# A fused retention and feed-forward kernel: the order of its late tasks, with the transpose of tile 14's x ahead of that of q and k of tile 20

## The chip, the cores and the metric

The kernel runs on one core of one Trainium2 chip. A core has five engines that run side by side: TensorE (PE in the profile; its weight loads are PEld), VectorE (DVE), ScalarE (ACT), GpSimd (POOL) and SyncE (SP). Each takes its instructions in the order in which the program gives them, and an instruction that waits holds all that stand behind it on the same engine. SyncE, ScalarE and GpSimd also issue transfers, which the core's 16 DMA engines carry out. Matrix products land in PSUM, which has eight banks here, and everything else lives in SBUF. The metric is the time of one execution on the device in microseconds, the median of several runs.

## What is computed

The reference has two parts: a recurrence over 768 positions for each of 4 sequences and 8 heads, and a feed-forward network with a layer norm over the joined heads.

```
gamma = 1.0 - 2.0 ** (-5.0 - np.arange(H))          # one decay per head
for t in range(S):
    state = gamma * state + einsum('bhd,bhe->bhde', k[:, :, t], v[:, :, t])
    y[:, :, t] = scale * einsum('bhd,bhde->bhe', q[:, :, t], state)
x = y.transpose(0, 2, 1, 3).reshape(B, S, H * D)    # 4 x 768 x 512
xn = (x - mean(x)) / sqrt(var(x) + 1e-06) * g_ln
out = x + maximum(xn @ w_ch1, 0.0) @ w_ch2          # 512 -> 2048 -> 512
```

## The kernel before

The 4 x 768 positions are cut into 24 tiles of 128 positions. Tiles 0 to 3 are the first chunks of the four sequences; tiles 4 to 8, 9 to 13, 14 to 18 and 19 to 23 are the five further chunks of each sequence in turn. Within a tile the recurrence is a masked product: scores of q and k, times a mask of decays, times v. Across tiles a state is carried, which the chunks of k and v build up in bank PD.

The whole program is a list of some thousand tokens, the string `ORDER`. A token names one task, and the tasks are emitted in the order of the list. So the list fixes the order of work on each engine and, with it, the order of each engine's queue of transfers; all waits between engines follow from what the tasks read and write. The part of a token behind `/` names the engine where there is a choice (A ScalarE, D or nothing VectorE, S SyncE), the part behind `//` the banks. The tokens that matter here, with the line by which the profile names their instructions:

- `k`, `q`, `v` (L362): GpSimd issues the load of a tile's k, q or v, and the type changes from fp32 to bf16 on the way. q and k of tiles from 7 on have 8 slots, v has 9. `gk`, `gq`, `gv` (L391) are gates: GpSimd copies one element of the loaded tile, so that its queue goes on only when the load has landed. `vg` (L482): GpSimd multiplies v by decays.
- `tr` (L405): SyncE issues a transpose by DMA of q and k of a tile together; `ex` (L525): the same for the normalized x of a tile, half as large, from `xn` into `xnt`. Both stand in one queue. `eq` (L411): VectorE scales the transposed q.
- `vis` (L420 and L426): for two tiles at once TensorE computes the scores into the banks X0 to X3 and the share of the carried state into Y0 and Y1. `am` (L433): VectorE applies the mask, one bank each, which frees the bank. `py` (L448): TensorE multiplies the masked scores by v, into Y0 and Y1. `pd` (L490): TensorE adds k and vg into PD. `pb` (L501 on ScalarE, L505 on VectorE) reads the state off PD.
- `bn` (L456, L457), `sr` (L587), `rt` (L596), `nb` (L591), `xg` (L600), `xc` (L472): mean and variance, the root and its reciprocal, the shift, the normalized x, and a copy of x.
- `m` (L550): four blocks of x times w1 into a bank; `r` (L561 or L563): the relu that empties it. `wg` (L608 on ScalarE, L610 on VectorE): w1 times g_ln. For the groups of tiles 16 to 19 and 20 to 23 (numbers 12 and 13) the first product of the network is done with seven products in place of eight, in the manner of Strassen and Winograd: `wm` (L631) and `xt` (L653) make the sums of w1 and x, `f` (L671) the products, `fs` (L685) and `fo` (L698) their sums, and `fq` (L703) and `fr` (L712 on ScalarE, L710 on VectorE) the relu.
- `z` (L568): the second product of tiles 0 to 7, `ad` (L576) the sum with x. Tiles 8 to 23 do the second product two by two with seven products as well: `tm` (L620) are the four sums of blocks of w2, done once on VectorE in bf16 over 128 x 2048 elements, `sa` (L726) the sums of the hidden values, `s` (L737) the products and `o` (L751) their sums with x. `st` (L583): ScalarE issues the store of a tile.

Products are grouped by tiles: group 8 is tiles 8 and 9, group 9 tiles 10 and 11, group 10 tiles 12 and 13, group 11 tiles 14 and 15. `m11_8`, the first product of group 11, needs the transposes `ex14` and `ex15`. The queue of SyncE around it, as far as it is given by the list, is

```
ex15/S tr18 tr19 tr20 ex14/S ex16/S tr21 ex17/S ex19/S ex18/S tr22 tr23
```

and the queue of GpSimd from the last loads of tile 21 on is

```
q21 v22 vg21 vg20 gk21 q22 q23 gv20 gq21 vg22 k22 k23 v23
```

Of the kernel before, what the change touches and what calls it, by code (L numbers as in the profile page):

```python
# [47 lines left out]
z2_3 ad0 tr10 gq10 z3_0//M v12 gk11 st0/A ad2 z3_1 tr11 eq8 q13 vis8//X2,X1,X3,X0 tm1 z3_2 am8b am9a
pd9 z3_3 vg11/ pb10/A am8a m7_12//X1 am9b vg10/ ad3 py9 r7_12/A py8 q12 z4_0//M bn8 xc9a gv11 z4_1
xc8b bn9 k13 z4_2 xc9b sr8 sr9 z4_3 rt8 rt9 nb8 nb9 eq10 xg8a m7_8//X0 xg8b ad4 xc8a ex8/S xg9b pd10  # L50
gv12 z5_0//M gv10 xg9a pb11 gk12 q14 r7_8/A z5_1 ex9/S eq11 gq11 k15 wg2/D pd11 vis10//X0,X1,X2,X3
tr12 pb12/A k14 z5_2 am11a sq6 v14 tr13 wg3/A am11b z5_3 rs6 vg12/ am10a py11 m7_4//X2 am10b gq13
vg2/ ad5 py10 m6_4//X0 xc11b bn11 gq14 z6_0//M r6_4/A bn10 pd12 gk15 gk13 z6_1 gq12 v13 pb13 sr10
sr11 st1/A z6_2 q15 rt10 r7_4/A rt11 nb10 nb11 wg1/D xg11a z6_3 v15 xg11b xg10a m8_14//X0 ex11/S ad6
gk14 gv14 xc10b vg14/ xc10a m8_8//X1 xc11a xg10b tr14 v16 r8_14/A eq12 pd2 z7_0//M eq13 r8_8/A tm2
ex10/S pb14/A vis12//X0,X1,X2,X3 gv13 z7_1 wg0/A am12a am12b pd14 m8_4//X0 gq15 tr15 k16 am13a py12
am13b m8_6//X1 k17 sq7 bn12 r8_4/A m8_12//X2 q16 tm4 sr12 r8_6/A py13 m8_2//X0 q17 xc12a r8_12/A
rt12 bn13 m8_0//X1 vg15/ xc13a xc13b nb12 m8_10//X2 r8_2/A gv15 gv16 eq14 xc12b k18 sr13 z7_2 xg12a
rt13 rs7 nb13 pb15 r8_10/A v17 z7_3 xg13a vg16/ r8_0/A m9_8//X0 ad7 xg13b xg12b pd15 eq15 ex13/S
s8_1//M sa8_1 r9_8/A pb16/A vis14//X0,X1,X2,X3 ex12/S st2/A s8_5 am14b tr16 gk18 am15a pd16 q20  # L60
m9_0//X1 am14a gk17 m9_12//X2 gq17 am15b tr17 gv17 gk16 k20 tm3 py14 py15 m9_10//X0 q18 st3/A r9_0/A
sa8_3 m9_6//X3 q19 r9_12/A bn15 st6/A m9_2//X1 k19 r9_6/A sa8_2 s8_2//X2 bn14 vg3/ r9_2/A xc15a
m10_2//X3 r9_10/A sa8_4 vg17/ xc14a sr14 m9_14//X0 o8_1 sr15 xc14b gq20 r10_2/A rt14 nb14 s8_6 pb17
xc15b r9_14/A rt15 s8_3 o8_2 gq18 nb15 eq16 xg15a m10_14//X0 xg15b o8_3 eq17 xg14b ex15/S m9_4//X1
v19 o8_4 r10_14/A wm3 xg14a s8_7 gq16 tr18 r9_4/A st4/A v18 pd17 vis16//X0,X1,X2,X3 o8_5 pb18/A
sa10_1 tr19 gk19 v20 s8_4 am16b am16a pd3 m10_12//X1 am17a py16 st5/A am17b m10_4//X0 xc16b o8_6
# [2 lines left out]
r10_10/A m10_8//X0 nb16 gk20 eq18 xg16a rt17 s10_2//X1 o10_1 xg16b q21 xc16a nb17 sa10_4 ex16/S
xc17b s10_6 r10_8/A o10_2 v22 xg17b eq19 s10_3 xg17a sa12_1 vis18//X0,X1,X2,X3 o10_3 vg21/ o10_4  # L70
pd19 am19b s10_7 pb20/A vg20/ am18b m11_8//X3 am18a gk21 q22 o10_5 m11_6//X1 r11_8/A am19a q23
sa12_3 py18 py19 pd20 m11_14//X0 bn19 tr21 gv20 pb21/A gq21 vg22/ s10_4 bn18 sr19 ex17/S k22 pd21
m11_4//X2 rt19 o10_6 sr18 r11_6/A rt18 nb19 sa12_2 xc18b s12_1//M r11_4/A nb18 k23 wm2 xg19a s12_5
xg19b v23 xg18a eq20 m11_0//X1 ex19/S xg18b o12_1 xc19b s12_2//X2 sa12_4 xc19a ex18/S xc18a r11_0/A
wm4 s12_6 pb22/A s12_3 eq21 r11_14/A o12_2 pd22 o12_3 vis20//X0,X1,X2,X3 o12_4 tr22 s12_7 am20b
pb23/A am20a f12_1_1//X1 am21a m11_2//PD fs12_1_1 xt12_1 f12_0_1//X0 am21b f12_1_5//X2 xt12_2
fs12_0_1 py20 o12_5 py21 fs12_1_5 m11_12//X3 xt12_3 tr23 r11_2/A bn21 f12_1_6 r11_12/A f12_0_2//PD
bn20 fs12_1_2 f12_0_6 m11_10//X3 xc20b fo12_0_1 sr20 fs12_0_2 rt20 f12_1_7 xt12_4 sr21 xc20a nb20
f12_0_5//PD eq22 xg20a f12_0_7 fo12_1_3 fs12_0_5 s12_4 rt21 xc21a eq23 r11_10/A nb21 fo12_0_3
f12_1_4 xg21a f12_1_2//X3 o12_6 xg21b f12_1_3 sa14_1 xg20b f12_0_4 xc21b fo12_1_1 ex20/S f12_0_3  # L80
fq12_1 fo12_1_2 s14_1//M fq12_0 sa14_2 st13/A ex21/S vis22//X0,X1,X2,X3 st12/A fo12_0_2 s14_5 am22b
am23b f12_3_5//PD f12_3_1//X1 am23a f12_2_1//X3 am22a f12_2_5//X2 st9/A fs12_3_5 py23 sa14_4 py22
fs12_2_1 s14_2//X0 bn22 fs12_2_5 f12_2_6 fs12_3_1 bn23 f12_3_3 fs12_2_2 f12_2_3 sr22 f12_3_6 o14_1
sr23 fr12_1_2/A f12_2_7 rt22 rt23 fs12_3_2 s14_6 nb22 fo12_2_2 xg22b fo12_2_3 f12_3_7 xc22a xc22b
f13_1_1//X2 fo12_3_2 xc23a xg22a s14_3 o14_2 nb23 ex22/S fo12_3_3 xg23a f12_2_4 xg23b o14_3
f13_0_2//X0 sa14_3 xc23b f13_0_1//PD ex23/S fr12_0_1/A f12_2_2//Y0 o14_4 f12_3_4 fo12_2_1 st11/A
s14_7 fq12_3 fr12_0_2/D fs13_0_1 f12_3_2//Y0 o14_5 fr12_1_1/A f13_2_1//X1 fo12_3_1 f13_1_2//Y1
xt13_1 s14_4 fs13_1_1 xt13_2 st14/A xt13_3 f13_0_5//Y0 fq12_2 o14_6 f13_0_6 st10/A fo13_1_1
f13_2_2//X3 fs13_0_5 fr12_3_1/D f13_1_5//M fs13_0_2 fo13_0_1 f13_0_3 fs13_1_5 f13_1_6 fo13_0_2
fr12_2_1/A f13_0_7 f13_3_1//X0 fo13_0_3 fs13_2_1 f13_3_2//Y0 sa16_1 fr12_3_2/A f13_1_3 f13_3_5//Y1  # L90
fs13_1_2 xt13_4 f13_2_6 fo13_2_1 fs13_3_1 f13_1_7 fo13_3_1 f13_2_5//X3 f13_3_6 fo13_1_3 s16_1//Y0
fo13_1_2 fs13_3_5 sa16_3 fs13_2_5 s16_5 fr13_0_1/A sa16_2 f13_3_3 o16_1 f13_2_3 fs13_2_2 f13_1_4
fs13_3_2 fo13_2_2 f13_2_7 fr12_2_2/A f13_3_7 fr13_1_1/A s16_6 fo13_3_3 fq13_1 fr13_2_1/D s18_1//M
fo13_2_3 fr13_1_2/A f13_3_4 sa16_4 s16_2//X2 fq13_3 sa18_1 fr13_3_2/A s16_3 sa18_3 fr13_2_2/A sa18_2
f13_0_4 f13_2_4 fo13_3_2 fq13_0 s18_5 o16_3 fr13_3_1/A sa18_4 s18_2//X0 o16_4 fq13_2 o18_1 s16_7
st15/A o16_2 s18_6 st16/A o16_5 fr13_0_2/D o18_2 s20_1//Y1 sa20_1 s16_4 sa20_2 s20_5 s22_1//PD
sa22_1 o20_1 s18_3 o16_6 s20_6 st17/A o18_3 sa20_4 s22_5 sa22_2 s20_3 s20_2//X0 sa22_4 o18_4
s22_2//X1 o20_3 o22_1 s18_7 o22_2 s22_6 o18_5 sa20_3 s22_3 o20_4 sa22_3 s18_4 o22_3 o20_2 s20_7
# [753 lines left out]
```

## Time and profile before

| | us |
|---|---|
| median of 3 runs | 207.11 |
| the three runs | 206.81, 207.11, 210.05 |
| the profiled execution | 204.79 |
| its span, from the first to the last instruction | 203.0 |

The profiled execution was shorter than the three runs, so numbers taken from its trace are differences, to be set against the median. TensorE is busy for 96% of the span, VectorE for 82%, ScalarE for 58% and GpSimd for 49%; a busy TensorE is not one at its peak, since a matmul's end is modelled. The granted clock of TensorE is 0.997 of full speed on the mean. The DMA engines carry loads of q, k, v and the weights until about 138 us; after that only x's last transposes and the stores remain.

Three views are used. The page gives busy time by engine and in slices of the span. The view of waits says which engine sat idle and what ended it. The timeline gives single instructions with start and length, and in square brackets the idle time ahead of one and what ended it. The name in such a bracket is inferred from semaphores: where the engine named had long been done, it was another.

### The profile page before, as it was taken

The numbers are of one execution on the slowest core, as the hardware profiler recorded it, in microseconds if no ns is written. First come the engines' busy times: TensorE is split into PE (matmuls) and PEld (weight loads), VectorE is DVE, ScalarE is ACT, GpSimd is POOL, SyncE is SP. The second block draws the span as 40 slices with busy tenths as digits, with TensorE's granted clock in tenths as the row PEclk, the third lists the DMA queues.
The fourth block names the chain that finished last, engine by engine and source line by source line (L and its number), as shares of the span: only waits on it lengthen the run. The fifth ranks groups of instructions, "written<-read, shape, count | busy, mean of one in ns | idle before, by whom it ended". The sixth has DMA issues, their size and how long they took to land.

```text
span 203.0 us, 5754 instructions
## 1 busy us (share of the span) xinstructions
PE 195.3 (96%) x2303; PEld 159.3 (78%) x2303; DVE 167.1 (82%) x386; ACT 117.0 (58%) x270; POOL 98.9 (49%) x145
## 2 busy tenths in 40 slices
...
GB/s 126 169 185 177 164 188 171 174 178 161 144 122 175 147 139 171 116 149 156 212 193 117 178 193 153 119 152 126 3 154 56 103 107 2 0 55 52 52 76 239
DMA packets 110478, 27.16 MB, mean 134 GB/s; under 512 B 103153, under 2 KB 107505, under 8 KB 110450
## 3 DMA queue, kind: packets, MB, share of 16 engines
...
## 4 chain that ended last, share of the span: by engine, by line
PE 45%; DMA 4%; ACT 2%; DVE 1%; ACTq 0%; issue 0%
PE M L737 11%; PE X L671 8%; PE X L550 7%; PE Y L737 5%; DMA xnt<-xn 4%; PE X L737 3%; PE PD L737 3%; PE PD L671 2%; PE Y L671 2%; PE X L420 1%; PE Y L448 1%; ACT xn L600 1%; ACT h L561 1%; PE PD L490 1%; PE Y L426 0%; PE M L671 0%
## 5 line engine op out<-in xcount | busy, mean ns | idle before, releaser
L550 PE MATMUL X<-xnt,w 128*128 128x128 bf16 (+1 forms) x760 | 62.9, 237 | 1.3 <-DMA xnt<-xn 1.3
L550 PEld LDWEIGHTS <-w 128*128 128x128 bf16 x768 | 53.8, 98 | 6.1 <-DMA xnt<-xn 1.6
L561 ACT ACTIVATE h<-X 128x512 bf16<-128x512 f32 x56 | 33.3, 608 | 17.9 <-PE X L550 17.7
L433 DVE TENSOR_TENSOR asb<-X,mask 128x512 bf16<-128x512 f32 x48 | 30.3, 681 | 1.8 <-PE X L420 1.5
L737 PEld LDWEIGHTS <-h 128*128 128x128 bf16 x256 | 24.8, 98 | 3.5 <-issue 0.5
L568 PE MATMUL M<-w,h 128*128 128x512 bf16 x96 | 23.0, 379 | 0.0
L472 ACT CAST x_all<-Y 128x256 bf16<-128x256 f32 (+1 forms) x39 | 15.0, 410 | 11.8 <-DVE xn L466 7.8
L482 POOL TENSOR_TENSOR vg<-v,vsc 128x512 bf16<-128x512 bf16 x16 | 16.7, 1047 | 10.1 <-DMA v<-in_v_dram 10.1
L568 PEld LDWEIGHTS <-h 128*128 128x128 bf16 x128 | 11.8, 98 | 11.8
L737 PEld LDWEIGHTS <-sum 128*128 128x128 bf16 x192 | 18.6, 98 | 2.2
L456 DVE BATCH_NORM_STATS2 bns<-Y 128x6 f32<-128x256 f32 (+1 forms) x39 | 16.1, 448 | 4.7 <-PE Y L448 4.5
L362 POOL DMA_DIRECT2D v<-in_v_dram x20 | 18.0, 901 | 3.3 <-DMA w<-in_moe_w_ch_dram 2.3
L501 ACT ACTIVATE state<-PD,gch 128x128 bf16<-128x128 f32 x40 | 11.6, 385 | 11.5 <-PE PD L490 10.6
L600 ACT ACTIVATE xn<-Y,shift,rstd 128x256 bf16<-128x256 f32 x32 | 16.5, 575 | 1.5 <-DVE shift L591 1.4
L362 POOL DMA_DIRECT2D qk<-in_k_dram x17 | 15.3, 903 | 0.7 <-issue 0.7
L362 POOL DMA_DIRECT2D qk<-in_q_dram x17 | 15.1, 894 | 0.8 <-issue 0.7
L726 DVE TENSOR_TENSOR sum<-h,sum 128x1024 bf16<-128x1024 bf16 x16 | 11.0, 688 | 1.0 <-PE Y L737 0.8
L391 POOL COPY scrap<-qk 1x1 bf16<-1x1 bf16 x28 | 8.1, 289 | 6.6 <-DMA qk<-in_k_dram 3.7
L737 PE MATMUL M<-w,h 128*128 128x256 bf16 x80 | 10.4, 272 | 0.4 <-ACT xn L600 0.3
L737 PE MATMUL M<-early,sum 128*128 128x256 bf16 x80 | 10.4, 273 | 0.0
L757 PE MATMUL PD<-zeros 128*128 128x512 bf16 (+1 forms) x33 | 9.2, 417 | 1.2 <-DVE zeros L271 1.2
L671 PEld LDWEIGHTS <-w 128*128 128x128 bf16 x96 | 9.4, 98 | 1.1
...
## 6 DMA issues: line engine op xcount, KB each, us to landing
...
```

The lines of the kernel that those rows point to most:

```text
L362: nc.gpsimd.dma_start(out=dst, in_=tok[kind][TILES[t]])
L433: nc.vector.tensor_tensor(out=slot(asb, t)[:, :, par, :], in0=bank(("pa", t, par)).rearrange("p (i t) -> p i t", t=P), in1=mask.rearrange( ...
L456: nc.vector.bn_stats(out=bns[:, t, i, :], in_=x)
L472: nc.scalar.copy(out=dst, in_=src)
L482: nc.gpsimd.tensor_tensor(out=slot(vgs, chunk(t)), in0=v_of(t), in1=vsc[:, c, :].unsqueeze(2).to_broadcast([P, H, D]), op=ALU.mult)
L501: nc.scalar.activation(out=slot(state, chunk(t) - 1)[:, i, :], in_=pd[:, i, :], func=AF.Copy, scale=gch[:, c - 1, i:i + 1])
L550: nc.tensor.matmul(bank(("mm", g, ho))[:, j * n * P:(j + 1) * n * P], lhsT=w1[:, ko, (ho + j) * P:(ho + j + 1) * P], rhs=x[:, x0:x0 + n, k ...
L561: nc.scalar.activation(out=dst, in_=src, func=AF.Relu)
L568: nc.tensor.matmul(bank(("m2", t)), lhsT=slot(h1, t // 4)[:, ho, t % 4 * P:(t % 4 + 1) * P], rhs=w2[:, ho, :], start=(ho == 0), stop=(ho = ...
L600: nc.scalar.activation(out=heads(slot(xns, t))[:, :, half], in_=split(y_of(t, half)), func=AF.Identity, bias=shift[:, t:t + 1], scale=rstd ...
L671: nc.tensor.matmul(f_bank(g, j, i)[:, n * w:(n + 1) * w], lhsT=f_left(i, ko)[:, (nb * j + n) * P:(nb * j + n + 1) * P], rhs=f_right(g, i)[ ...
L737: nc.tensor.matmul(product(t, i), lhsT=left(t, i)[:, ho, :], rhs=right[i][:, ho, :], start=(ho == 0 and i in (1, 2)), stop=(ho == HK - 1), ...
```

## The change

Only `ORDER` changes, from the token `z2_3` on, which stands at 59 us in the trace. The 752 tokens behind it are the same tasks in another order; the code that emits them is untouched. Twelve of them change engine and 53 change bank. From VectorE to ScalarE go wg2, pb17, fr12_0_2, fr12_3_1 and fr13_0_2; from ScalarE to VectorE go pb12, fr12_1_2, fr12_2_1, fr13_0_1, fr12_2_2, fr13_1_1 and fr13_3_1. As named by its author, the order was searched anew over latencies of transfers from nine traces, with the sums of w2 on VectorE (`tm`) charged longer than before.

The lines of the diff that hold `tr20` and `ex14`:

```diff
...
-gv19 r10_12/A vg19/ bn16 m10_10//X2 st8/A st7/A tr20 py17 sr16 m10_6//X1 pb19/A rt16 sa10_2 ex14/S
...
+vis16//X0,X1,X2,X3 tr19 o8_5 s8_4 am16a ex14/S am16b pd3 m10_4//X0 o8_6 st5/A am17a gv19 pb19/A
+vg19/ py16 m10_6//X1 bn16 st7/A m10_12//X2 tr20 xc16a am17b sr16 s10_1//M rt16 wm1 r10_12/A gv18
...
```

Of the rest only the parts that are spoken of are shown, as the queues of the single engines read off the two lists (the engine and the bank of a token left out):

```diff
 TensorE, 78 to 95 us
-z6_0 pd12 z6_1 z6_2 z6_3 m8_14 m8_8 pd2 z7_0 vis12 z7_1 pd14 m8_4 py12 m8_6 m8_12 py13 m8_2 m8_0 m8_10 z7_2 z7_3 m9_8 pd15 s8_1
+z6_0 pd12 z6_1 z6_2 z6_3 m8_8 m8_14 z7_0 vis12 pd2 z7_1 m8_6 m8_2 py13 py12 m8_12 pd14 m8_4 m8_0 m8_10 z7_2 z7_3 m9_8 pd15 s8_1
 VectorE, 83 to 96 us
-tm2 am12a am12b am13a am13b bn12 tm4 rt12 bn13 nb12 eq14 rt13 rs7 nb13 pb15 ad7 eq15 sa8_1
+tm2 am12b am12a am13a am13b bn13 bn12 rt13 nb13 rt12 tm4 eq14 nb12 pb15 ad7 eq15 sa8_1
 SyncE, from 70 us on
-ex8 ex9 tr12 tr13 ex11 tr14 ex10 tr15 ex13 ex12 tr16 tr17 ex15 tr18 tr19 tr20 ex14 ex16 tr21 ex17 ex19 ex18 tr22 tr23 ex20 ex21
+ex9 ex8 tr12 tr13 ex10 tr14 tr15 ex11 ex13 ex12 tr16 tr17 ex15 tr18 tr19 ex14 tr20 ex17 ex16 tr21 ex18 ex19 tr22 tr23 ex21 ex20
 GpSimd, 64 to 82 us
-vg11 vg10 q12 gv11 k13 gv12 gv10 gk12 q14 gq11 k15 k14 v14 vg12 gq13 vg2 gq14 gk15 gk13 gq12 v13 q15 v15 gk14 gv14 vg14 v16
+gv11 vg10 q12 k13 vg11 q14 gq11 gv10 k15 v14 gk12 vg12 gv12 k14 vg2 gk15 gq14 gq13 gk13 gq12 v13 q15 v15 gk14 gv14 v16 vg14
 GpSimd, from 119 us on
-q21 v22 vg21 vg20 gk21 q22 q23 gv20 gq21 vg22 k22 k23 v23
+q21 v22 gk21 vg21 vg20 vg22 q22 q23 k23 v23 gv20 gq21 k22
 TensorE, 121 to 138 us
-s10_3 vis18 pd19 s10_7 m11_8 m11_6 py18 py19 pd20 m11_14 s10_4 pd21 m11_4 s12_1 s12_5 m11_0 s12_2 s12_6 s12_3 pd22 vis20 s12_7
+s10_3 vis18 pd19 s10_7 m11_8 py18 s10_4 m11_14 py19 pd20 m11_4 m11_0 pd21 s12_1 s12_5 s12_2 m11_6 s12_6 s12_3 vis20 pd22 s12_7
 ScalarE, stores among its tasks, 95 us on
-st2 st3 r9_0 r9_12 st6 ... st4 pb18 st5 xc16b r10_12 st8 st7
+st2 st3 r9_10 pb17 ... st4 r10_14 r10_2 pb18 st5 pb19 st7 ... st6 ... st8
```

More of the change, by code (lines that the diff above doesn't have):

```diff
@@ L47 @@
 z2_1 gk9 q10 q11 gv9 eq9 rs5 rs3 pb9 r7_0/A r6_12/A r6_0/A z2_2 z0_1 gq9 v11 v10 z0_2 vg9/ z0_3 k12
[L48 to L66, printed above, removed]
-gv19 r10_12/A vg19/ bn16 m10_10//X2 st8/A st7/A tr20 py17 sr16 m10_6//X1 pb19/A rt16 sa10_2 ex14/S
-s10_1//M sa10_3 r10_6/A gv18 bn17 r10_4/A m10_0//X3 v21 xc17a wm1 s10_5 sr17 gq19 r10_0/A k21
@@ L69 @@
[L69 to L98, printed above, removed]
@@ L99 @@
-o22_4 o18_6 st22/A s22_7 o20_5 st18/A st20/A s20_4 st19/A o22_5 st23b/A s22_4 o20_6 st21/A o22_6
-st23a/A
+z2_3 ad0 tr10 gq10 z3_0//M v12 gk11 st0/A ad2 z3_1 tr11 eq8 q13 vis8//X2,X1,X3,X0 tm1 pd9 z3_2 am9a
+z3_3 am8a gv11 am9b m7_8//X2 vg10/ am8b py9 ad3 r7_8/A py8 q12 bn9 z4_0//M k13 bn8 z4_1 sr9 pb10/A
+vg11/ z4_2 rt9 nb9 sr8 sq7 rt8 xg9b z4_3 nb8 xg8b q14 pd10 xc8b ad4 m7_12//X0 xg9a gq11 gv10 xg8a
+pb11 ex9/S k15 z5_0//M xc9a r7_12/A eq10 xc9b z5_1 ex8/S eq11 xc8a sq6 st1/A pd11 wg2/A
+vis10//X0,X1,X2,X3 pb12 tr12 z5_2 v14 am11b tr13 am11a z5_3 gk12 vg12/ am10a wg3/A m6_4//X2 am10b
@@ new lines @@
+gv12 k14 ad5 py11 py10 m7_4//X0 vg2/ rs7 bn11 z6_0//M r6_4/A gk15 gq14 bn10 gq13 gk13 gq12 pd12 v13
+z6_1 xc11b pb13 sr11 xc10b q15 sr10 z6_2 r7_4/A rs6 rt11 rt10 nb11 nb10 wg1/D v15 xg11b z6_3 xg10b
+xc11a m8_8//X0 xg11a ad6 xg10a m8_14//X1 xc10a eq12 ex10/S r8_8/A eq13 z7_0//M gk14 gv14 r8_14/A v16
+tm2 wg0/A tr14 vis12//X0,X1,X2,X3 pd2 z7_1 am12b vg14/ am12a tr15 m8_6//X1 gv13 k16 am13a m8_2//X0
+am13b ex11/S r8_6/A gv15 k17 pb14/A py13 py12 m8_12//X1 vg15/ bn13 xc12a pd14 r8_2/A m8_4//X2 gv16
@@ new lines @@
+bn12 gq15 q16 sr13 r8_12/A m8_0//X0 rt13 q17 sr12 nb13 xc12b rt12 tm4 xc13a m8_10//X1 xg13a k18
+r8_4/A z7_2 xg13b v17 eq14 r8_10/A z7_3 ex13/S nb12 vg16/ pb15 xg12a m9_8//X1 r8_0/A ad7 xg12b pd15
+eq15 xc13b s8_1//M ex12/S r9_8/A sa8_1 pb16/A vis14//X0,X1,X2,X3 sa8_2 s8_5 st2/A tr16 am15b am15a
+pd16 gk18 q20 m9_2//X3 am14b tr17 gk17 m9_10//X2 am14a gq17 gv17 gk16 k20 sa8_3 py15 st3/A m9_14//X0
+wm3 r9_10/A q18 pb17/A py14 m9_6//X1 q19 bn15 r9_2/A m9_12//X2 k19 r9_14/A sa8_4 xc14b m9_4//X3
+r9_6/A bn14 vg17/ sr15 s8_2//X0 xc14a r9_4/A rt15 gq20 vg3/ nb15 o8_1 sr14 m9_0//X1 xg15b rt14 nb14
@@ new lines @@
+tm3 s8_6 r9_0/A xc15a s8_3 xc15b eq16 gq18 r9_12/A xg15a m10_14//X1 o8_3 v19 xg14b ex15/S o8_4
+m10_2//X2 xg14a sa10_1 gq16 st4/A v18 r10_14/A o8_2 pd17 tr18 s8_7 eq17 r10_2/A gk19 v20 pb18/A
+vis16//X0,X1,X2,X3 tr19 o8_5 s8_4 am16a ex14/S am16b pd3 m10_4//X0 o8_6 st5/A am17a gv19 pb19/A
+vg19/ py16 m10_6//X1 bn16 st7/A m10_12//X2 tr20 xc16a am17b sr16 s10_1//M rt16 wm1 r10_12/A gv18
+r10_4/A py17 m10_0//X2 r10_6/A bn17 v21 xc17a m10_8//X0 xc16b sa10_2 sr17 gq19 k21 s10_5 rt17 sa10_3
+r10_8/A xc17b gk20 nb16 m10_10//X1 nb17 st6/A sa10_4 xg16b o10_1 q21 s10_2//X0 r10_10/A eq18 r10_0/A
@@ new lines @@
+v22 s10_6 o10_2 xg17a sa12_1 xg16a s10_3 eq19 xg17b vis18//X0,X1,X2,X3 ex17/S o10_3 o10_4 pd19 am18a
+s10_7 ex16/S pb20/A gk21 vg21/ am18b m11_8//X0 o10_5 vg20/ am19b py18 s10_4 am19a bn18 m11_14//X1
+tr21 vg22/ o10_6 py19 sr18 pd20 q22 r11_8/A rt18 m11_4//X2 bn19 pb21/A q23 m11_0//X0 nb18 eq20
+r11_4/A sa12_2 pd21 sr19 k23 s12_1//M xg18a rt19 sa12_3 r11_0/A s12_5 nb19 v23 xg18b wm2 xg19b
+ex18/S s12_2//X0 gv20 xc18b gq21 k22 xc18a o12_1 r11_14/A m11_6//X2 sa12_4 st8/A xg19a o12_2 s12_6
+r11_6/A eq21 ex19/S xc19a wm4 s12_3 xc19b pb22/A vis20//X0,X1,X2,X3 o12_3 o12_4 pd22 am20a s12_7
@@ new lines @@
+pb23/A am20b m11_12//X0 am21a tr22 am21b py20 r11_12/A f12_1_1//X1 o12_5 f12_0_1//X2 xt12_1 py21
+fs12_0_1 m11_2//X0 xt12_2 tr23 bn20 fs12_1_1 f12_1_5//X3 xc20a r11_2/A f12_1_6 xt12_3 fs12_1_5 bn21
+f12_0_2//PD m11_10//X0 sr20 xc21a fs12_1_2 fo12_0_1 f12_0_6 sr21 r11_10/A f12_1_7 rt21 rt20 xt12_4
+fs12_0_2 f12_0_5//PD nb21 sa14_1 s12_4 fs12_0_5 nb20 fo12_1_3 xg20a f12_0_7 eq23 xc20b f12_1_4 xg20b
+o12_6 f12_1_2//X0 fo12_0_3 xg21a f12_1_3 xg21b fo12_1_1 f12_0_4 fq12_1 ex21/S f12_0_3 fo12_1_2
+fq12_0 s14_1//M eq22 xc21b fr12_1_1/A fo12_0_2 ex20/S vis22//X0,X1,X2,X3 sa14_2 s14_5 am23a am22a
@@ new lines @@
+f12_3_5//PD f12_3_1//X2 am23b f12_2_1//X0 st9/A am22b fs12_3_1 f12_2_5//X3 py23 sa14_4 fs12_2_5 py22
+f12_3_6 sa14_3 xc22b s14_2//X1 fs12_3_5 bn23 fs12_2_1 f12_2_3 fs12_3_2 f12_3_3 o14_1 xc23a f12_3_7
+xc23b sr23 bn22 f12_2_6 s14_6 rt23 o14_2 sr22 fs12_2_2 s14_3 rt22 nb23 nb22 fo12_3_3 xg22b f12_2_7
+xg22a o14_3 f13_0_2//X1 xc22a ex22/S o14_4 xg23a f12_3_4 fo12_2_2 xg23b s14_7 fr12_0_1/A fo12_2_3
+ex23/S f12_3_2//X3 fo12_3_2 st10/A f13_1_2//Y0 o14_5 fr12_3_2/A f12_2_2//Y1 fo12_3_1 fq12_3
+f13_0_1//PD fo12_2_1 s14_4 st11/A fs13_0_1 f13_1_1//X2 o14_6 f12_2_4 xt13_1 fs13_1_1 f13_3_1//X3
```

12 lines of the change are left out of this document (added).

## The prediction

> **What bounds the kernel now.** I read the page first, then sums by stage, then what TensorE waited for. The change begins at the token z2_3, at 59 us, so only what lies behind it counts.
>
> ```profile
> span 203.0 us, 5754 instructions
> PE 195.3 (96%) x2303; PEld 159.3 (78%) x2303; DVE 167.1 (82%) x386; ACT 117.0 (58%) x270; POOL 98.9 (49%) x145
> core 0: us, PE busy (x) PEld busy (x) DVE busy (x) ACT busy (x) POOL busy (x), PEclk, DMA share, GB/s
> 62.00:95.00 33.00, 32.97 (x380) 22.75 (x380) 30.20 (x71) 24.94 (x63) 26.85 (x43) 1.00 1.83 150
> 95.00:126.00 31.00, 29.50 (x368) 25.81 (x367) 28.01 (x63) 20.36 (x54) 18.69 (x30) 1.00 1.57 175
> 160.00:183.00 23.00, 23.00 (x213) 20.62 (x211) 20.41 (x39) 17.84 (x30) 0.00 (x0) 1.00 0.17 53
> PE X L550 <- DMA xnt<-xn: 1.3, 1, 1.3
> PE M L737 <- ACT xn L600: 0.3, 1, 0.3
> ```
>
> The first number of a window row is its length, the second TensorE's busy time. From 62 to 183 us TensorE is busy all but some 1.5 us, and the view of waits names two events: 1.3 us for a transpose by DMA, and 0.3 us. The order of tokens leaves the number and shape of matmuls alone, so these two, 1.66 us together (1.35 and 0.31 below), are all that it can win where TensorE sets the pace. The first is reached so:
>
> ```profile
> 108.59 1.19 SPq L525 DMA_TRANSPOSE xnt<-xn  x1
> 109.38 0.58 ACT L600 ACTIVATE xn<-Y,shift,rstd 128x256 bf16<-128x256 f32 x1
> 109.95 8.61 SPq L405 DMA_TRANSPOSE tr<-qk  x3
> 118.66 3.25 SPq L525 DMA_TRANSPOSE xnt<-xn  x2
> 118.66 7.49 DMA xnt<-xn
> 126.19 1.05 PE L550 MATMUL X<-xnt,w 128*128 128x256 bf16 x8 [1.35 <-DMA xnt<-xn]
> ```
>
> These are SyncE's queue (ex15; tr18 to tr20; ex14 and ex16), the activation that completes x of tile 14 (xg14a, done at 109.96), the piece of the chain, and m11_8, the first product that needs tile 14. x lay ready 8.7 us before its transpose was issued: three transposes of q and k stood ahead of it, and the transpose then took 7.49 us to land.
>
> **The change, part by part.**
>
> *ex14 ahead of tr20.* The three tr take 8.61 us of SyncE's queue, 2.87 each on the mean, so ex14 is issued about 2.9 us earlier, and needs 1.35. ex15, the other half of m11_8's input, stays ahead of it; its last activation, xg15a, now follows r9_0, xc15 and r9_12, which may move it by some 1 us either way, and it was issued 10 us ahead of need. tr20 comes later by one ex (3.25 / 2 = 1.6 us); its user, vis20, stands 10 us behind m11_8. What is late next is vis18, which needs tr19; that has the same rank as before. I take the whole wait as gone: -1.35. Bounds: 0 (landing limited by the transfers ahead in any case) to -1.35.
>
> *The order around 85 us.* The rows are VectorE's sum tm2, its four am12/am13, TensorE's pd14 and m8_4, then rt13, ad7 and s8_1:
>
> ```profile
> 83.30 2.20 DVE L620 TENSOR_TENSOR early<-w,early 128x2048 bf16<-128x2048 bf16 x1
> 83.39 1.03 POOL L482 TENSOR_TENSOR vg<-v,vsc 128x512 bf16<-128x512 bf16 x1
> 85.43 2.47 DVE L433 TENSOR_TENSOR asb<-X,mask 128x512 bf16<-128x512 f32 x4
> 85.83 0.39 PE L490 MATMUL PD<-vg,qk 128*128 128x128 bf16 x4
> 86.16 1.03 PE L550 MATMUL X<-xnt,w 128*128 128x256 bf16 x8
> 92.77 0.16 DVE L596 RECIPROCAL rstd<-rstd 128x1 f32<-128x1 f32 x1 [0.70 <-ACT rstd L587]
> 94.47 0.75 DVE L576 SCALAR_TENSOR_TENSOR osb<-M,rstd,x_all 128x512 f32<-128x512 f32 x1
> 95.28 1.03 PE L737 MATMUL M<-w,h 128*128 128x256 bf16 x8 [0.31 <-ACT xn L600]
> L620 DVE TENSOR_TENSOR early<-w 128x2048 bf16<-128x2048 bf16 x1 | 1.2, 1217 | 0.0
> ```
>
> Before, pd14 stood between z7_1 and m8_4. After, pd2 (behind vis12) and pd14 (behind m8_12) leave that place, and m8_6 into X1 comes at once, at 85.83. X1 is free when am12b, now first of the four, is done: 85.43 plus a quarter of 2.47 and its tail, about 86.1. So TensorE waits some 0.33 us. Behind it py13 now precedes py12 and needs am13, the last of the four, done at 87.9; two products of 0.87 us from 86.16 end there too: nothing more. The 0.31 at 95.28: s8_1 overwrites bank M, which ad7 read until 95.22; the activation named is not what it needs. In the new order the same VectorE work precedes ad7, but bn13 and bn12 come first and tm4 stands behind rt13, so that the 0.70 us that VectorE idled ahead of rt13 are filled; ad7 then starts up to 0.7 us sooner, as soon as z7_3 is done, and this wait goes: -0.31. Together +0.02; bounds -0.31 to +0.4.
>
> Which length has tm2? Its own row says 2.20, a like sum (tm1, last row) 1.22. The Trainium skill (SBUF — State Buffer, SBUF: two separate sides) says that VectorE with two SBUF inputs and a GpSimd operation that reads SBUF exclude each other for a whole instruction. The trace agrees here: 1.22 plus vg14's 1.03 is 2.25. In the new order v16's load stands between gv14 and vg14, so by that rule tm2 takes 1.22, am12b is done a microsecond earlier and the 0.33 is not paid. I keep 2.20, tm2's own row.
>
> *GpSimd's queue, late part.* Rows: the wait for v12, then v22's load, vg21 and vg20, gk21, q22 and q23, vg22, k22 and k23, SyncE's tr22 (which waits for k22), TensorE's pd22, vis20 and s12_7:
>
> ```profile
> 71.00 0.41 POOL L391 COPY scrap<-v 1x1 bf16<-1x1 bf16 x2 [2.64 <-DMA v<-in_v_dram]
> 108.00:110.00 2.00, 2.00 (x21) 1.79 (x19) 1.92 (x4) 2.00 (x6) 2.00 (x5) 1.00 0.27 17
> 120.41 0.88 POOL L362 DMA_DIRECT2D v<-in_v_dram  x1
> 124.80 2.04 POOL L482 TENSOR_TENSOR vg<-v,vsc 128x512 bf16<-128x512 bf16 x2 [3.51 <-DMA v<-in_v_dram]
> 126.79 0.64 POOL L391 COPY scrap<-qk 1x1 bf16<-1x1 bf16 x1
> 127.37 1.82 POOL L362 DMA_DIRECT2D qk<-in_q_dram  x2
> 129.55 1.03 POOL L482 TENSOR_TENSOR vg<-v,vsc 128x512 bf16<-128x512 bf16 x1
> 130.54 1.81 POOL L362 DMA_DIRECT2D qk<-in_k_dram  x2
> 135.98 2.68 SPq L405 DMA_TRANSPOSE tr<-qk  x2
> 136.72 0.39 PE L490 MATMUL PD<-vg,qk 128*128 128x128 bf16 x4
> 137.04 0.62 PE L420 MATMUL X<-trq,tr 64*128 64x128 bf16 x16
> 137.85 1.03 PE L737 MATMUL M<-w,h 128*128 128x256 bf16 x8
> DMA to landing us min/median/max: 3.6/6.5/9.8
> ```
>
> This part speaks against the change. Before, q22, q23, vg22, k22, k23, v23 followed vg20; after, it is gk21, vg21, vg20, vg22, q22, q23, k23, v23, gv20, gq21, and k22 last. From vg22's start to k22's issue that is 1.03 + 1.82 + 1.82 + two gates of 0.2, 5.1 us. k22 then lands 3.6 us (the least of all loads) to 5.44 (130.54 to 135.98) later. pd22 reads k22 and holds TensorE's whole queue. It stood at 136.72; less the 1.35, plus vis20's 0.81, now ahead of it, TensorE arrives at 136.2. If vg22 starts where it did, at 129.55, k22 lands at 138.2 to 140.1: a wait of 2.0 to 3.9. But loads go earlier. The 2.64 us wait for v12 held q14, k15, k14 and v14; in the new order q14, k15 and v14 precede it, and each later gate waits for a landing, so the lead is handed on. Transfers have room for it: 17 GB/s from 108 to 110. Leads of 2 and 3 us put vg22 at 127.5 and 126.5, and k22 at 136.2 to 138.0 and 135.2 to 137.0. I take 2.5 us and a landing near 4.7: k22 at 136.8, a wait of 0.6; bounds 0 and 3.9. pd20 needs vg20, now behind gk21: at worst 1.2 us (126.79 + 0.2 + 2.04 against TensorE's arrival, 128.41 in the chain less 1.35 plus one product of 0.87), by the same lead nothing; it is not added, since a wait there shortens that at pd22.
>
> *Engines exchanged.*
>
> ```profile
> L608 ACT ACTIVATE w<-w,gcol 128x512 bf16<-128x512 bf16 x8 | 5.2, 765 | 0.0
> L610 DVE TENSOR_SCALAR w<-w,gcol 128x512 bf16<-128x512 bf16 x8 | 3.7, 516 | 0.0
> L712 ACT ACTIVATE h<-h 128x1024 bf16<-128x1024 bf16 x6 | 6.4, 1068 | 0.0
> L710 DVE TENSOR_SCALAR h<-h 128x1024 bf16<-128x1024 bf16 x2 | 0.8, 418 | 0.0
> ```
>
> wg2 moves to ScalarE: 5.2 / 2 = 2.6 us there in place of 1.8 on VectorE. With wg3 ScalarE works 5.1 us on end there; its row for 62 to 95 us shows 8 us idle to catch up in. pb12 moves the other way, pb17 to ScalarE. Of the nine relu that change sides six go to VectorE, four of them of 1024 elements (4 x 0.42), three come back; VectorE gains about 1.3 us between 160 and 183 us, where its row shows 2.6 idle. Two stores of early tiles (st6, st8) go later on ScalarE's queue, which leaves room for the transposes around 115 us. All of this lies beside TensorE: 0. Should VectorE's slack not fall where it is needed, 0.3 us. At the end the same two products, sums and stores come last: 0.
>
> **Sum.** -1.35 + 0.02 + 0.60 + 0 = -0.73. The profiled execution took 204.79 us (span 203.0 and 1.8 around it), the median of three runs is 207.11; I put the difference on the median: 206.4.
>
> **The rivals.**
> 1. *k22 comes late (other side).* The lead is lost again: with k22 at 140.1, 3.9 + 0.02 - 1.35 = +2.6, 209.7 us. From a landing after 137.5 on, the change loses. For it: the 3.51 us that GpSimd already waited for v21, and the 5.1 us of work now ahead of k22. Against it: 17 GB/s at 108 us and the removed 2.64.
> 2. *All waits go.* tm2 at 1.22, k22 by 136.2: -1.66, 205.4 us. This is the end of what order can give.
> 3. *The change doesn't do what it says.* ex14 lands no sooner, or another transpose takes its place as the last (tr19 for vis18, ex11, now behind ex10, tr14 and tr15, for m9_8): about 207.1. Against it: x ready 8.7 us early.
> 4. *A long wait costs the clock.* The granted clock stays 1.00 through waits of 1.35 us; none here is longer. If 3.9 us halve it for as long again, 1.9 us are added to rival 1: 211.6. The Trainium skill (TensorE: Matmul & The Clock Gate, Part 1: The HAM clock gate) puts the idle window behind which the clock is halved at about 3.4 us; no run here shows it.
>
> **Chances.** Forecast (net gain 0.2 to 1.3, 205.8 to 206.9) 0.42; rival 1 (207.1 to 209.7) 0.25; rival 2 0.18; rival 3 0.11; rival 4 0.04. The forecast's own range is 205.8 to 206.9. For 8 in 10, 205.0 (rival 2 and 0.4 of scatter between runs) to 208.8 (most of rival 1). 2% of 207.11 is 4.1 us, about what a measurement of this kernel can tell from no change. No mechanism wins more than 1.7 us, so faster gets 0.02, for scatter; slower, above 211.25, is rival 4 and a sum of small waits: 0.05; within 2% 0.93.
>
> **What would show it.** m11_8 with no idle time and ex14 issued near 115 us: first step right. A gap ahead of m8_6 with tm2 at 2.2: second; no gap and tm2 at 1.2: the rule of the port. A gap at pd22 that ends with k22's landing, and of what size: third. Idle time of TensorE behind 139 us would refute the zeros. TensorE's idle time unchanged in sum, at other places, would make the prediction wrong in its gain; over 3 us more of it, in its sign.

## The result and the profile after

The changed kernel is slower: 211.39 us median of six runs (210.8 to 215.3) against 206.96 (205.8 to 210.1) for the kernel before on the same chip, a ratio of 1.030 with a 95% interval of 1.025 to 1.036, or 4.4 us. The forecast was 206.4, the range 205.0 to 208.8. Ratios and intervals, here and below, leave out runs more than 1.5% above the fastest of their kernel, so they can differ a little from the ratio of the medians. The profiled execution of after took 215.30, the longest of its runs, and two of its waits are not in most other traces; so a second trace of the same kernel, 209.87 us, is read beside it ("the second trace" below).

The page of after: the span, the engines, TensorE's granted clock in 40 slices, and the chain that ended last.

```profile
span 213.5 us, 5749 instructions
PE 197.9 (93%) x2303; PEld 160.8 (75%) x2303; DVE 167.9 (79%) x385; ACT 115.9 (54%) x271; POOL 98.7 (46%) x145
PEclk9999999999999999999999999995999999999998
PE 39%; DMA 29%; POOL 23%; issue 6%; ACT 1%; DVE 0%; POOLq 0%; ACTq 0%
```

TensorE's busy share is down from 96% to 93%. A slice of the clock's row is 5.3 us: in the one that begins at 144 us the granted clock is 0.5. The chain is now half made of DMA and GpSimd, where before had 4% of DMA and no GpSimd: the work that ended last hangs on a load.

What TensorE waited for in after, 55 to 214 us (total, times, longest), and its stretches around 145 us in the columns of the prediction's rows:

```profile
PE PD L489 <- DMA qk<-in_k_dram: 3.8, 1, 3.8
PE PD L489 <- POOL vg L481: 1.7, 1, 1.7
PE X L549 <- DMA xnt<-xn: 1.6, 1, 1.6
...
139.00:142.00 3.00, 2.17 (x45) 1.72 (x43) 2.62 (x5) 1.85 (x7) 0.14 (x1) 1.00 2.30 153
142.00:145.00 3.00, 0.02 (x1) 0.02 (x2) 1.70 (x3) 0.00 (x0) 0.00 (x0) 0.74 1.38 77
145.00:148.00 3.00, 3.00 (x17) 2.25 (x18) 0.56 (x2) 1.14 (x4) 0.00 (x0) 0.50 0.57 105
148.00:151.00 3.00, 3.00 (x31) 2.39 (x30) 0.72 (x2) 0.78 (x2) 0.00 (x0) 0.62 0.38 73
151.00:154.00 3.00, 3.00 (x30) 2.69 (x28) 2.77 (x8) 3.00 (x9) 0.00 (x0) 1.00 0.02 5
160.00:183.00 23.00, 23.00 (x246) 20.66 (x241) 21.25 (x47) 15.80 (x33) 0.00 (x0) 1.00 0.25 73
```

Line numbers of the changed kernel are one less than before's. The first row is pd22, which waits 3.8 us for k22. The third is m9_8 and ex11. In the windows from 145 us TensorE is busy all the time, and its granted clock, the number behind GpSimd's, is 0.50 and 0.62. The missing clock from 142 to 151 adds up to (0.26 + 0.50 + 0.38) x 3 = 3.4 us, that is 6.8 us at half speed. About 1.5 us of it, those ahead of 145 us, fall into the wait and cost nothing. Behind 151 us TensorE is never idle.

The timeline of the pieces of that chain: GpSimd's gate gk21, vg21 vg20 vg22 in one row, q22 q23, k23, v23 and, behind two short gates, k22; SyncE's tr22, which waits for k22, and tr23; TensorE's vis20, pd22 and s12_7.

```profile
130.56 0.18 POOL L390 COPY scrap<-qk 1x1 bf16<-1x1 bf16 x1 [4.89 <-DMA qk<-in_k_dram]
130.70 3.29 POOL L481 TENSOR_TENSOR vg<-v,vsc 128x512 bf16<-128x512 bf16 x3
133.94 1.81 POOL L361 DMA_DIRECT2D qk<-in_q_dram  x2
135.74 0.89 POOL L361 DMA_DIRECT2D qk<-in_k_dram  x1
136.61 0.90 POOL L361 DMA_DIRECT2D v<-in_v_dram  x1
...
138.25 0.88 POOL L361 DMA_DIRECT2D qk<-in_k_dram  x1
...
145.09 2.66 SPq L404 DMA_TRANSPOSE tr<-qk  x2
...
140.78 0.40 PE L425 MATMUL Y<-state,trq 64*128 64x64 bf16 x16
144.98 0.61 PE L489 MATMUL PD<-vg,qk 128*128 128x128 bf16 x4 [3.81 <-DMA qk<-in_k_dram]
145.38 1.91 PE L736 MATMUL M<-w,h 128*128 128x256 bf16 x8
```

k22 is issued at 138.25, behind four other loads of the last five microseconds, and has landed when tr22 and pd22 start at 145: 6.8 us after its issue. TensorE had arrived at 141.2. Behind the wait the eight products of s12_7 take 1.91 us; before, they took 1.03.

To compare traces that began the changed part at different times, times are also counted from TensorE's first eight products into bank M (the row of 1.89 us at 60.09 before, 61.71 after, 59.69 in the second trace) to the end of its last product: 139.1 before, 147.4 after, 144.0 in the second trace.

### The profile page after: what moved, and what is told of

Same layout as the page of the kernel before. It is cut to its first block, busy times and chain, and to the rows that moved or that the text cites. A ratio compares the mean times of both kernels' runs of the same rounds, so it can differ in the third digit from the quotient of the medians.

```text
span 213.5 us, 5749 instructions
## 1 busy us (share of the span) xinstructions
PE 197.9 (93%) x2303; PEld 160.8 (75%) x2303; DVE 167.9 (79%) x385; ACT 115.9 (54%) x271; POOL 98.7 (46%) x145
## 4 chain that ended last, share of the span: by engine, by line
PE 39%; DMA 29%; POOL 23%; issue 6%; ACT 1%; DVE 0%; POOLq 0%; ACTq 0%
DMA qk<-in_k_dram 10%; DMA v<-in_v_dram 10%; POOL qk L361 8%; PE X L549 8%; PE X L670 8%; PE M L736 6%; PE Y L736 5%; POOL vg L481 5%; DMA mid<-in_v_dram 5%; DMA qk<-in_q_dram 4%; POOL scrap L390 3%; POOL v L361 3%; PE PD L736 2%; PE X L736 2%; PE PD L670 2%
## 5 line engine op out<-in xcount | busy, mean ns | idle before, releaser
L549 PE MATMUL X<-xnt,w 128*128 128x128 bf16 (+1 forms) x768 | 64.8, 238 | 2.1 <-DMA xnt<-xn 1.6
L560 ACT ACTIVATE h<-X 128x512 bf16<-128x512 f32 x57 | 33.8, 610 | 29.5 <-PE X L549 29.3
L567 PE MATMUL M<-w,h 128*128 128x512 bf16 x96 | 22.9, 379 | 0.2 <-DVE osb L575 0.2
L567 PEld LDWEIGHTS <-h 128*128 128x128 bf16 x128 | 11.9, 98 | 12.3 <-issue 0.3
L481 POOL TENSOR_TENSOR vg<-v,vsc 128x512 bf16<-128x512 bf16 x16 | 17.6, 1106 | 6.8 <-DMA v<-in_v_dram 6.8
L599 ACT ACTIVATE xn<-Y,shift,rstd 128x256 bf16<-128x256 f32 x32 | 17.0, 583 | 1.4 <-DVE shift L590 1.2
L390 POOL COPY scrap<-qk 1x1 bf16<-1x1 bf16 x28 | 6.1, 219 | 13.7 <-DMA qk<-in_k_dram 9.6
L725 DVE TENSOR_TENSOR sum<-h,sum 128x1024 bf16<-128x1024 bf16 x16 | 11.7, 731 | 0.2
L736 PE MATMUL M<-w,h 128*128 128x256 bf16 x80 | 11.2, 287 | 0.0
L489 PE MATMUL PD<-vg,qk 128*128 128x128 bf16 x52 | 5.3, 226 | 5.5 <-DMA qk<-in_k_dram 3.8
```

Of the source, the lines that this page charges most:

```text
L390: nc.gpsimd.tensor_copy(out=scrap, in_=old[0:1, 0, 0:1])
L481: nc.gpsimd.tensor_tensor(out=slot(vgs, chunk(t)), in0=v_of(t), in1=vsc[:, c, :].unsqueeze(2).to_broadcast([P, H, D]), op=ALU.mult)
L549: nc.tensor.matmul(bank(("mm", g, ho))[:, j * n * P:(j + 1) * n * P], lhsT=w1[:, ko, (ho + j) * P:(ho + j + 1) * P], rhs=x[:, x0:x0 + n, k ...
L560: nc.scalar.activation(out=dst, in_=src, func=AF.Relu)
L567: nc.tensor.matmul(bank(("m2", t)), lhsT=slot(h1, t // 4)[:, ho, t % 4 * P:(t % 4 + 1) * P], rhs=w2[:, ho, :], start=(ho == 0), stop=(ho = ...
L599: nc.scalar.activation(out=heads(slot(xns, t))[:, :, half], in_=split(y_of(t, half)), func=AF.Identity, bias=shift[:, t:t + 1], scale=rstd ...
```

## The experiments

All kernels are one of the two lists with a few tokens moved; a ratio stands where the runs give an interval.

**Is it the tail of GpSimd's queue?** a_again is after once more. a_tail gives after the eleven last tasks of GpSimd in before's order, b_tail gives before those in after's order.

```diff
 a_tail (b_tail: the reverse, in before)
-gk21 vg21 vg20 vg22 q22 q23 k23 v23 gv20 gq21 k22
+vg21 vg20 gk21 q22 q23 gv20 gq21 vg22 k22 k23 v23
```

> The changed kernel once more, for a trace on this chip beside the others. Two theories. T1: k22, the last load in GpSimd's new order, lands late; TensorE waits for it at pd22 (3.8 us in the profile of after), idles so long that its clock is halved for some microseconds (2.4 us lost), and pd20 waits 1.7 us because vg21 and vg20 stand behind the gate gk21. T2: the new order of the transfers from 64 us on makes all of them late, and pd22 is only the last place where it shows. Both expect 211.4 within 0.6; T1 expects the wait at pd22 to end with k22's landing and to be 2 us or more in each run.

> The changed kernel, but GpSimd's last eleven tasks (from gk21 on) in the order of before: vg21 vg20 gk21 q22 q23 gv20 gq21 vg22 k22 k23 v23. T1: the waits at pd20 and pd22 and the clock's dip go, 206.0 to 207.2, at or below the kernel before. T2: waits of 3 us or more stay somewhere behind 120 us, 209.5 or more.

> The kernel before, but the same eleven tasks in the order of after, k22 last. T1: pd22 waits 2.0 to 3.9 us and the clock dips: 209 to 212. T2: under 208, since the transfers ahead are those of before.

Medians of four runs each: a_again 210.28 (209.87 to 210.72), a_tail 206.24 (203.75 to 208.01), b_tail 208.64 (207.48 to 209.14), the kernel before 205.76. The seven runs of before scatter from 202.6 to 211.5. These eleven tasks carry most of the loss, 4.5 us between the medians of a_again and before: taken out they win 4.0 us, put into before they lose 2.9, to 208.6 where 209 to 212 was expected. In b_tail the long wait does not stand at pd22, where it was expected. TensorE's timeline and stretches of b_tail:

```profile
129.91 0.58 PE L489 MATMUL PD<-vg,qk 128*128 128x128 bf16 x4 [3.51 <-POOL vg L481]
...
128.00:130.00 2.00, 0.09 (x2) 0.09 (x2) 0.32 (x2) 0.00 (x0) 2.00 (x3) 0.80 0.28 48
130.00:132.00 2.00, 2.00 (x13) 1.47 (x13) 0.05 (x1) 1.41 (x7) 2.00 (x3) 0.50 0.81 151
132.00:134.00 2.00, 2.00 (x19) 1.69 (x18) 0.73 (x5) 0.84 (x3) 2.00 (x3) 0.84 1.18 75
```

This is pd20, which needs vg20, and vg20 stood behind the gate gk21, which waited 4.9 us for k21. What TensorE waited at pd20, it did not wait again at pd22 (0.6). So the same cause has two doors: whichever product of PD meets the late queue first pays. The clock drops here too, for (0.20 + 0.50 + 0.16) x 2 / 0.5 = 3.4 us.

**Is part of it the clock?** a_fill keeps the wait at pd22 and fills it with work: 16 products of zeros, accumulated to PD, ahead of pd22.

```diff
+    @on("fill")
+    def _(eng, n):
+        for _ in range(n):
+            nc.tensor.matmul(BANK["PD"][:, 0:4 * P], lhsT=zeros[:, 0:P], rhs=zeros[:, 0:4 * P],
+                             start=False, stop=False, skip_group_check=True)
...
-vis20 pd22 s12_7
+vis20 fill16 pd22 s12_7
```

> The changed kernel with 16 more products of zeros by zeros, 128x512, added to bank PD right ahead of pd22 (they add nothing to the sums; 3.5 us of TensorE at full clock), so that TensorE works where it would idle. If the idle time is what halves the clock: granted clock 1.00 behind pd22, eight products in 0.87 us there, and some 2 us less than the changed kernel on the same chip, 209.0 to 209.8, though the wait for k22 ends at the same time. If the slow products behind pd22 have another cause, they stay slow and the time is that of the changed kernel or above.

Median 208.91 (206.37 to 211.05, four runs), too wide a scatter for a verdict by the time. The clock tells it: its mean over the four runs is 0.995 to 1.000, where the six runs of after have 0.979 to 0.988 and the four of a_again 0.979 to 0.992. The traces show the place. Stretches of the second trace, then of a_fill, and a_fill's pd22 and s12_7:

```profile
136.00:139.00 3.00, 0.00 (x0) 0.00 (x0) 2.08 (x4) 0.00 (x0) 0.00 (x0) 0.90 1.39 96
139.00:142.00 3.00, 2.79 (x16) 2.11 (x17) 0.42 (x1) 1.14 (x4) 0.00 (x0) 0.50 0.49 90
142.00:145.00 3.00, 3.00 (x22) 2.25 (x21) 0.85 (x2) 0.60 (x1) 0.00 (x0) 0.50 0.46 87
```

```profile
136.00:139.00 3.00, 3.00 (x19) 1.57 (x18) 1.72 (x3) 0.00 (x0) 0.00 (x0) 1.00 0.68 64
139.00:142.00 3.00, 3.00 (x41) 2.73 (x40) 1.28 (x3) 1.88 (x6) 0.00 (x0) 1.00 1.16 145
...
138.59 0.39 PE L489 MATMUL PD<-vg,qk 128*128 128x128 bf16 x4
138.81 1.04 PE L736 MATMUL M<-w,h 128*128 128x256 bf16 x8
```

With the fill the clock stays 1.00, and s12_7 takes 1.04 us, not the 1.91 of after. From pd22's start to the end of the last product it takes 61.6 us in a_fill (138.59 to 200.19), 64.5 in the second trace (139.21 to 203.71), 64.2 in after. So the halved clock costs 2.9 and 2.6 us. That agrees with the 6.0 and 5.2 us that TensorE worked at half clock behind the wait, of which half is lost.

**Which move of the tail?** a_k22 undoes one: k22 stands right behind v22, all else is after. a_early brings all five last loads there and vg21 and vg20 ahead of gk21. b_early brings the five loads there in before.

```diff
 a_k22
-v22 gk21 vg21 vg20 vg22 q22 q23 k23 v23 gv20 gq21 k22
+v22 k22 gk21 vg21 vg20 vg22 q22 q23 k23 v23 gv20 gq21
 a_early
+v22 k22 q22 q23 k23 v23 vg21 vg20 gk21 vg22 gv20 gq21
 b_early
+v22 k22 q22 q23 k23 v23 vg21 vg20 gk21 gv20 gq21 vg22
```

> The changed kernel with one task moved: the load of k22 stands right behind that of v22, in front of the gate gk21, instead of last. T1 (k22's rank is the cause): k22 lands near 127 to 132, pd22 does not wait for it, the clock stays 1.00; vg21, vg20 and vg22 keep their place behind gk21 and start at most 0.9 us later, so pd20 may wait 0 to 2 us. 5 us less than the changed kernel: 205 to 206.5 if before is at 206, no slower than before by more than 0.5. T2 (all transfers late): the wait moves to q22, k23 or v23, 209 or more.

> The changed kernel with all five last loads (k22 q22 q23 k23 v23) right behind v22, where GpSimd stood idle 3 to 5 us, then vg21 vg20 gk21 vg22. T1: no wait at pd22, at pd20 at most what the landing of v21 costs; the gain that the forecast gave the rest of the change shows: 1 to 2 us below before. T2: the five loads share the DMA engines with tr20, ex17 and ex16 and delay those: waits at vis18 or m11_8, no gain.

> The kernel before with the five last loads right behind v22 and nothing else. T1: before has no wait for them (pd22 stood where k22 had landed), so 0 to 0.5 us either way, and where a run of before is slow by a late k22 or v22, that goes. The rival: before's spread between runs (202.6 to 211.5) comes from these loads, then the median is 1 us or more below before.

With 12 runs each and the kernel before at 206.43: a_k22 206.12, ratio 0.998 (0.993 to 1.003); a_early 205.99, 0.997 (0.993 to 1.001); b_early 206.46, 1.005 (1.000 to 1.009). One token moved undoes the loss. GpSimd's k22 in a_k22, and TensorE's pd22:

```profile
124.17 0.90 POOL L361 DMA_DIRECT2D qk<-in_k_dram  x1
...
138.94 0.40 PE L489 MATMUL PD<-vg,qk 128*128 128x128 bf16 x4
```

k22 is issued 14.8 us ahead of pd22 there, and pd22 waits for nothing. The two early kernels show the price of going too far: five loads are 4.4 us of issues on GpSimd, the pair vg21 and vg20 starts 2.3 us later in a_early than in the second trace and 3.4 later in b_early than in before, and pd20 waits 1.9 us in a_early and 2.6 in b_early. Neither wait moved the clock. The gain of 1 to 2 us that was expected of a_early did not come.

**Is the first step worth what was forecast?** b_ex14 is before with ex14 and tr20 exchanged, nothing else.

```diff
-tr19 tr20 ex14/S
+tr19 ex14/S tr20
```

> The kernel before with only ex14 and tr20 exchanged on SyncE. T1: the one wait at m11_8 (1.35 us in the profile of before) goes and nothing takes its place: 1.0 to 1.5 us below before. The rival: the wait at pd20 or pd22, which lie behind it and move up by what is won, takes it back: within 0.4 us of before.

205.97 against 206.43, ratio 0.998 (0.994 to 1.002): no gain that 12 runs can see. What TensorE waited for in b_ex14, and its m11_8:

```profile
PE M L737 <- DVE osb L751: 0.6, 2, 0.4
PE PD L490 <- DMA qk<-in_k_dram: 0.4, 1, 0.4
PE PD L490 <- POOL vg L482: 0.2, 1, 0.2
PE X L420 <- ACT h L561: 0.2, 1, 0.2
PE X L420 <- DVE trq L411: 0.2, 1, 0.2
PE X L550 <- DMA xnt<-xn: 0.2, 1, 0.2
...
125.61 1.91 PE L550 MATMUL X<-xnt,w 128*128 128x256 bf16 x16
```

m11_8 waits for nothing, as the step said, and starts 0.65 us earlier behind the first products into bank M than in before; the wait of 0.2 us for xnt stands at 103 us. But the list adds up to 1.8 us, as much as before's (1.66). Of these, 0.6 us stand behind m11_8, for vg20 and k22, where TensorE now comes earlier. The other 1.3 stand ahead of m11_8, 0.6 of them ahead of ex14's issue at 114.9 us, so the exchange did not cause those; whether it caused the rest is open.

**Is it where pd22 stands, or when k22 lands?** a_pd22late leaves GpSimd's list as it is in after and puts pd22 and what reads PD behind it (pb23) later.

```diff
-vis20 pd22 s12_7 m11_12 py20 f12_1_1 f12_0_1 py21
+vis20 s12_7 m11_12 py20 f12_1_1 f12_0_1 pd22 py21
```

> The changed kernel, GpSimd's order untouched, but pd22 five tasks later on TensorE (behind f12_0_1, some 3 us of work) and its reader pb23 behind fs12_1_1. T1: k22 lands as late as before, but what it holds is less: a wait of 0 to 1.5 us at pd22 in place of 3.7, no dip of the clock, 3 to 5 us less than the changed kernel, 206 to 207.5. If the whole stretch is late for another reason, the wait only moves and 209.5 or more stays.

205.77 in 10 runs against 205.98, ratio 1.002 (0.997 to 1.007). TensorE in a_pd22late, f12_0_1 and pd22:

```profile
139.36 1.04 PE L670 MATMUL X<-xnt,w 128*128 128x256 bf16 x8
140.24 0.39 PE L489 MATMUL PD<-vg,qk 128*128 128x128 bf16 x4
```

k22 lands as late as ever (tr22 at 140.09, 6.2 us behind the issue), but TensorE has other work to do until then and does not wait for it. The load's lateness is free here; the place of its user is what costs.

**Where did the lead go?** A guess was that the transposes, which the new order brings forward too, take it: SyncE issues ex10, tr14 and tr15 ahead of ex11. a_ex11 puts them back as before.

```diff
-ex10 tr14 tr15 ex11
+ex11 tr14 ex10 tr15
```

> The changed kernel with only SyncE's ex11 back ahead of tr14, ex10 and tr15, as before. The forecast had a lead of the loads of 2.5 us at v22, and the traces show 4 us at k16 and none at v18. L1: the lead is lost to the four transposes issued together there; then k18 and v22 land 1 to 2 us earlier (taken from z2_3), the wait at pd22 falls to 2 or less and the time to 208 to 209. L2: it is lost in GpSimd's own order (gv15, gv16 and gq15 ahead of q16): no change at pd22, 210 to 211.

211.36 in four runs, ratio 1.027 (1.019 to 1.036), and pd22 still waits 3.6 us, with 3.4 us of halved clock behind it. The guess falls. The traces say where the lead was lost: behind the first products into bank M, k16 was issued 2.2 to 4.0 us earlier than in before, but v22, which stood at 60.3 us there, at 60.5 in the second trace, 61.6 in a_ex11 and 63.1 in after. That GpSimd's own order does it (gates for v tiles ahead of that for q16) would fit, but was not tried alone.

**Together.** a_best is after with three moves: k22 behind v22, vg21 and vg20 ahead of gk21, and the order of a_ex11. b_best is before with ex14 ahead of tr20 and k22 behind v22.

> The changed kernel with k22 right behind v22, vg21 and vg20 ahead of gk21, and ex11 ahead of tr14: every wait over 0.5 us that the traces of it showed (m9_8, pd20, pd22) is addressed. If TensorE's waits are all that is left: 1.0 to 1.7 us below before, 204.7 to 205.4 where before is 206.4. If what is won in one place is lost at the next transfer: 205.8 to 206.4, no difference.

> The kernel before with two steps: ex14 ahead of tr20, and k22 right behind v22. 1.0 to 1.5 us below before if the waits at m11_8 and pd22 set the time; 0 to 0.5 if the transfers only exchange who waits.

a_best 204.17, ratio 0.995 (0.991 to 0.999); b_best 204.73, ratio 0.993 (0.988 to 0.998), 12 runs each against 205.98. By the ratios both are 1.0 to 1.4 us faster than before; the intervals end just under 1. a_best's only listed wait of TensorE:

```profile
PE X L419 <- DVE trq L410: 0.6, 1, 0.6
```

Its span is 202.4 us. So with the loads in place the rest of the new order shows no more worth than two exchanges in the old one. The profiled execution of b_best took 212.16 us, far above its median; only its waits and its clock are read, in the last section.

## Why the prediction was wrong

**The failing step: "I take 2.5 us and a landing near 4.7: k22 at 136.8, a wait of 0.6."** Everything in this sentence can now be set beside the traces. Times are from the first products into bank M; vg22 is taken 2.0 to 2.2 us behind the start of its row of three, as two of them take; the flight is from k22's issue to tr22's. In before tr22 stood behind transposes that ended at 135.80 us, so the flight there is at most 5.4.

| | before | forecast | after | second trace | a_ex11 |
|---|---|---|---|---|---|
| vg22 starts | 69.5 | 67.0 | 71.1 | 67.4 | 68.2 |
| k22 is issued | 70.5 | 72.0 | 76.5 | 72.5 | 73.3 |
| k22's flight | 5.4 | 4.7 | 6.8 | 7.1 | 7.0 |
| TensorE stands at pd22 | 76.6 | 76.1 | 79.5 | 75.9 | 76.6 |
| it waits there | 0 | 0.6 | 3.8 | 3.65 | 3.6 |

The flight is wrong in these three traces, by 2.1 to 2.4 us. The prediction quoted a median of 6.5 for such loads and a maximum of 9.8, and still took 4.7, short of k22's own 5.44, as if k22 flew alone; but the change puts it last behind q22, q23, k23 and v23. That these lengthen its flight is likely, not shown: the DMA share, the last number but one of a window's row, is 2.30 from 139 us on in after and 2.51 from 134 us on in the second trace, against 1.89 from 134 us on in before; but in b_tail, where k22 followed the same loads, if some half a microsecond later, it took 4.7 us, as forecast. The view of transfers from 128 to 150 us groups the two loads of k, first in before, then in after (KB each, median us from issue to landing):

```profile
qk<-in_k_dram POOLq DMA_DIRECT2D x2, 128.0 KB, 4.9
```

```profile
qk<-in_k_dram POOLq DMA_DIRECT2D x2, 128.0 KB, 6.7
```

The lead is wrong in its mechanism. vg22 starts 2.1 us earlier in the second trace, nearly as taken, 1.3 in a_ex11, and 1.6 later than before in after. But it was to come from earlier loads, and v22 came no earlier. vg22 gained its place because q22 and q23 (1.82 us) and two gates no longer stand ahead of it, which the prediction did not count; against that worked the gate gk21, now ahead of vg21, which waited 3.6 to 4.9 us for k21. That the number came out near 2 once is luck. With the median flight of 6.5 and the lead as taken, the same sum gives k22 at 138.6 and a wait of 2.4: by the prediction's own bound, 137.5, a loss. The row was shown in the prediction and not used. The measured waits, 3.6 to 3.8 us, are longer still, and the clock, below, comes on top.

**The clock (rival 4) was priced apart from the wait (rival 1).** It got 0.04 beside 0.25. The traces allow no such choice at the upper end: waits of 3.5, 3.6, 3.65 and 3.8 us all brought the halved clock. The prediction put rival 1's upper price at 3.9 us; the upper part of it should have carried rival 4 with it, which at 211.6 is where the time came out. That the two agree so closely is in part luck: the wait was a little shorter than 3.9 us, and the price of the clock, 1.9, was low, since TensorE worked 5.2 and 6.0 us at half clock, not 3.9, which cost 2.6 and 2.9.

**The first step, ex14 ahead of tr20,** was right at its place: m11_8 does not wait in after, nor in any kernel of its order. It failed in "I take the whole wait as gone: -1.35" for the time: "what is late next" was looked up for SyncE's queue alone, and b_ex14 shows the next waits behind m11_8 on GpSimd's, for vg20 and k22, a few tenths each; with those that stand ahead of it they make up for what was won.

**The order around 85 us** came out as the rule set beside it said, not as the sum had it. VectorE's tm2 and GpSimd's vg14 in after:

```profile
85.36 1.22 DVE L619 TENSOR_TENSOR early<-w,early 128x2048 bf16<-128x2048 bf16 x1
81.78 1.06 POOL L481 TENSOR_TENSOR vg<-v,vsc 128x512 bf16<-128x512 bf16 x1
```

vg14 had run by then, tm2 took 1.22, and no wait of TensorE ahead of m8_6 is in the list, whose two rows not shown are 0.3 at vis12 and 0.2 ahead of a product of L567. In a_tail, where tm2 and vg14 did collide (last section), m8_6 waited 0.76 us for the mask, so the sum's case is real, at over twice its 0.33. The 0.31 at s8_1 is gone too, as forecast.

**The engines exchanged and the tail** were rightly put at zero: no idle time of TensorE behind 151 us in after.

**pd20** was bounded by 1.2 us "at worst", "by the same lead nothing". With k22 last it waited nothing in two traces and 0.5, 0.7 and 1.7 us in three, and 3.5 in b_tail. **Rival 3's** second part, ex11 late for m9_8, cost 1.6 us in after and in a_k22, and nothing in the others.

**The sum.** The second trace stands 4.9 us above before between the two marks (144.0 to 139.1). The wait at pd22 is 3.65, the clock 2.9, two small waits 0.8; before's two waits, 1.66, are gone. That makes 5.7, or 0.8 too much. Between the marks TensorE's idle time rose by 3.0 (from 1.7 to 4.7), as the waits say, and its busy time by 1.9 (from 137.4 to 139.3), where the clock alone would give 2.9; so the 0.8 lies in the busy time, and stays open. The forecast had 0.02 + 0.6 - 1.35 for the same places. The mechanism was named (rival 1, "k22 comes late", up to 3.9 us, and rival 4, the clock); the forecast's own sum took 0.6 us for the one and nothing for the other.
